# Token tiles of GT in two groups of addresses, with k's results between them

## The chip, the cores and the metric

The kernel runs on one NeuronCore of a Trainium2 chip. TensorE (PE) does the matrix products, VectorE (DVE) and ScalarE (ACT) the element-wise work, GpSimd (POOL) and SyncE (SP) issue transfers between the core's on-chip memory and DRAM, each in the order of its own queue. The metric is the device time of one execution in microseconds, as the median of several runs.

## What is computed

A gated mix of two blocks over 2048 tokens of width 640. The first is a linear attention with 32 heads of 20; the second is a gated linear unit.

```python
x = A_x
g = _sigmoid((x * gate_w).sum(-1, keepdims=True))
a = _A_ref(x, A_wqkv, A_wo)      # linear attention
b = _B_ref(x, B_w_gate, B_w_up, B_w_down)
return g * a + (1 - g) * b

# inside _A_ref
pq, pk = phi(q), phi(k)          # phi(t) = where(t > 0, t + 1, exp(t)) + 1e-6
kv = jnp.einsum("bhsd,bhse->bhde", pk, v)
z = jnp.einsum("bhsd->bhd", pk)
num = jnp.einsum("bhqd,bhde->bhqe", pq, kv)
den = jnp.einsum("bhqd,bhd->bhq", pq, z)[..., None] + 1e-6
o = num / den                    # then o @ wo

# inside _B_ref
h = _sigmoid(x @ w_gate) * (x @ w_up)
return h @ w_down
```

## The kernel before

Every product of two float32 operands is done as three matmuls of a high and a low part (`mm3`, L407 to L409); the parts come from `split`: ACT copies the high part (through `act`, L420) and DVE subtracts it from the source (through `vec2`, L424). All loads and stores go through `Ring.dma_start` (L364), on SP's queue (`sp`) or POOL's (`gp`).

**First stage (pool `p1`).** The keys are made block by block: 8 blocks of two times 128 tokens (`KPlain`, `KBlock`, each with a side 0 and a side 1). ACT and DVE turn a block's product into phi(k) in a tile `kr` or `kb` (`phi_a`, `phi_b`), and POOL adds that tile to `zacc` in memory by an accumulating transfer (`z_add`, L975). `k_split` writes the two parts of phi(k), and `split_xn` the two parts of x, into a *token tile* `tok` of 4 x 640 numbers per partition. Two tiles are used at the start to stage the weights of k (`st`); after them come sixteen token tiles, one for each block and side.

`GTBatch` multiplies x's transpose with phi(k) over a group of token tiles and adds the product to `gt`. The groups are block 0, blocks 1 and 2, blocks 3 and 4, blocks 5 and 6, and, as `glast`, block 7 alone (L1232). The last products of `glast` are the last reads of any token tile; DVE adds them to `gt` (L1245 and L2462).

**Second stage.** `p1` is closed at L1246, and its addresses go to other pools, which are opened with `reuse_waits="tile"`: the first write to a tile waits for the work on those earlier tiles whose bytes it takes, and for no others. On the left, from p1's first byte, comes `mp` (L1545): the operands of M (`wv_sb`, `wo_sb`, `kvt`, `kvh`, `kvl`, `woh`, `wol`). On the right come `pz`, `pw` and `pw2` (L1167, L1248, L1250): the weight tiles of the next products (`ws`, `wu`, `wst`) and their temporaries (`c`, `t`).

SP's queue then issues, in this order: `load_w()` (L1544), which fills a `wst` with the weights ("q", 1, 0); `load_mv(0)`, `load_mv(1)` and `load_mv(2)`, which fill three `wv_sb`; `load_mo(0)`, a `wo_sb`; `load_form(("q", 1, 2), 2)`, a `ws`; `load_mo(1)`, the second `wo_sb`; and `load_form(("q", 1, 2), 1)`, a `wu` (L1640 to L1647). An instruction of SP's queue that waits holds all behind it.

PE goes on with `q_phase(1, ...)` (L2213), which multiplies x with the weights of q in steps. The list `extra` (L2465) hangs other work on these steps: `kv_part(hg)` (L1608) multiplies `wv_sb` with columns of `gt` for a group of heads (L1613, in plain float32), DVE masks the product into `kvt`, `kvh` and `kvl`, and a further `wv_sb` is loaded; `wo_split(hg)` splits a `wo_sb` and loads the one for hg + 2; `m_part(hg)` multiplies both, and the result `ms` is stored to `m_dram` through POOL. `kv_part(0)` and `kv_part(1)` stand right behind the first two steps, whose five products use weights that were loaded earlier. `m_part(4)` takes its result out of PSUM with DVE (`vec_copy`, L860), the others with ACT.

**How the order comes about.** The class `Order` keeps a model of the engines' time while the program is written down, and places the work of ACT and DVE between PE's products. It knows of a tile that its buffer was used before by the tile `bufs` places earlier under the same tag (`place`, L204). It knows nothing of addresses that pools share, except where a line tells it so, such as L1543 and L1641, which set `sp.t`. Each engine then follows its list; semaphores make it wait for what it really needs.

**Where things lie.** The sizes below are bytes per partition and follow from the shapes in the code; the tags of a pool lie in the order in which they first appear. Counted from p1's first byte:

| who | before |
|---|---|
| `ta`, 2 buffers | 0 to 2,624 |
| `kr`, 5 buffers of 2,592 | 2,624 to 15,584 |
| `tok`, 6 buffers of 10,240 | 15,616 to 77,056 |
| `wv_sb` x3, `wo_sb` x2 | 0 to 12,320 |
| `kvt`, `kvh`, `kvl`, `woh`, `wol` | 12,320 to 26,400 |
| `wst`, 2 buffers of 5,120 | 30,976 to 41,216 |
| `ws` of `pw` | 46,336 to 55,552 |
| `wu`, 2 buffers of 3,072 | 55,552 to 61,696 |
| `c`, 5 buffers, and `t`, 4 | 61,696 to 80,128 |

The first three rows are p1's, the others take the same bytes later. At p1's end the six buffers of `tok` hold, in the order of their addresses: block 6 side 0, block 7 side 1, block 7 side 0, block 5 side 1, block 5 side 0, block 6 side 1.

Of the kernel before, what the change touches and what calls it, by code (L numbers as in the profile page):

```python
# [7 lines left out]
F32 = mybir.dt.float32  # L8
F32R = mybir.dt.float32r
# [5 lines left out]
P = 128  # L15
S, D, F = 2048, 640, 1536
# [6 lines left out]
HW = HALF + 2  # L23
# [351 lines left out]
def gated_mix_kernel(ctx: ExitStack, tc: tile.TileContext, xt, xn, wk, wv, wo, wst_q, wst_f, out_t):  # L375
# [111 lines left out]
    p1_cm = tc.tile_pool(name="p1", bufs=1)  # L487
    p1 = p1_cm.__enter__()

    def token_tile(dt=F32R):  # L490
        return p1.tile([P, 4, D], dt, name="tok", tag="tok", bufs=6)

    p1.tile([P, HW], F32, name="first", tag="ta", bufs=2)
    warm = nc.const_aps.tensor(1.0, (P, 512), mybir.dt.bfloat16)
# [179 lines left out]
    chunks = [Chunk(pr, c, xc, 0, xst_v) for pr in range(2) for c in range(TG // CW)]  # L674
    chunks[0].b12 = (b12h, b12l)
    xt_dram = dram.tile([P, 4, 2, 2, CW], F32, name="xt_dram")
    k3h, k3l = (p1.tile([P, 2, HW], F32R, name=n, tag="kr", bufs=5) for n in ("k3h", "k3l"))
    p1.tile([P, 8], F32, name="shift")
    st = [token_tile(F32).rearrange("p a b -> p (a b)") for _ in range(2)]
    wk_st = [st[k // 3][:, k % 3 * 2 * HW:(k % 3 + 1) * 2 * HW] for k in range(KC)]  # L680

    nc.scalar.dma_start(wk_st[0][:, :HW], wk[:P, :HW])
    for k in range(KC):
# [150 lines left out]
    def split_xn(n):  # L834
        i = tok(n // 2, n % 2)
        if i not in TOK:
            TOK[i] = token_tile()
        XN[i] = (TOK[i][:, 0], TOK[i][:, 1])
        split(*XN[i], xn_st.pop(n)[0])
        order.then(lambda: load_xn(n + 3))  # L840
# [118 lines left out]
    def k_split(i, after=""):  # L959
        r = KR.pop(i)  # L960
        if i not in TOK:
            TOK[i] = token_tile()
        PK[i] = (TOK[i][:, 2], TOK[i][:, 3])
        vh, vl = (t.rearrange(view2, j=2) for t in PK[i])
        act(vh, r, AF.Copy, after, bias=EPS)
        at = order.act + A_LAG

        def low():
            order.vec = max(order.vec, at)
            vec3(vl, r, EPS, f32(vh), OP.add, OP.subtract)  # L970
        order.then(low)
# [2071 lines left out]
```

## Time and profile before

| what | value |
|---|---|
| runs shown | 729.92, 731.73 and 733.86 us |
| median of the runs | 731.73 us |
| the profiled execution | 731.62 us |
| its span, first to last instruction | 729.9 us |
| mean granted TensorE clock in it | 0.998 |
| DMA, mean over the span | 263 GB/s, 191.95 MB |

The span is shorter than the profiled execution's time by 1.7 us, which lie around it. Times in the trace count from the span's start. In a timeline a row gives the start, the length, the engine, the line, the operation and its tiles; the bracket at its end is the time that the engine stood idle just before, and what ended that. A line is often that of a helper (L407 to L409, L420, L424, L364), so the tiles tell which work it is. SPq stands for SP's queue, PEld for PE's weight loads.

### The profile page before, as it was taken

The page shows a single profiled execution, that of the slowest core. Times are in us where ns is not written, and L with a number is a line of the kernel's source. Part 1 is how long each engine was busy: PE and PEld are TensorE (multiplying, and loading weights), DVE is VectorE, ACT ScalarE, POOL GpSimd, SP SyncE. Part 2 cuts the span into 40 slices and gives each one's busy share as a digit, 9 for nine tenths or more (in the row PEclk, how much of TensorE's full clock was granted, in tenths as well). Part 3 has the DMA queues.
Part 4 walks back from the last instruction along what each step waited for, and adds up shares of the span by engine and source line. Part 5 has one row for each costly group of instructions (what it writes and reads, how often), then busy time and mean ns, then how long its engine had stood idle before and what let it go on. Part 6 is the DMA issues. An engine that isn't in the chain of part 4 may idle for free.

```text
span 729.9 us, 9895 instructions
## 1 busy us (share of the span) xinstructions
PE 720.1 (99%) x3395; PEld 607.7 (83%) x3395; DVE 587.3 (80%) x1016; ACT 370.6 (51%) x685; POOL 116.9 (16%) x189
## 2 busy tenths in 40 slices
PE   9999999899899999999999999999999999999998
PEld 8999998788688888888888888888888888888886
DVE  6888888975778889898989988347696968799895
ACT  5774749247555763535354855345424241544451
POOL 0211021212310221311111133001010111002300
PEclk9999999999999999999999999999999999999999
DMA  8677679598867866767787979978979895959957
GB/s 253 161 208 202 177 192 287 129 323 284 294 232 269 311 231 241 260 223 263 280 293 287 311 255 336 414 264 268 360 244 293 284 389 180 408 215 336 223 104 237
DMA packets 81961, 191.95 MB, mean 263 GB/s; under 512 B 12234, under 2 KB 40346, under 8 KB 78198
## 3 DMA queue, kind: packets, MB, share of 16 engines
q1 hardware_dynamic: 60726, 117.72, 49.4%
q0 software_dynamic: 20896, 73.36, 30.1%
q8 instruction: 27, 0.44, 0.2%
q10 hardware_dynamic: 288, 0.23, 0.1%
q14 instruction: 24, 0.20, 0.1%
HBM read 113.46 MB, written 75.52 MB: 259 GB/s over the span
## 4 chain that ended last, share of the span: by engine, by line
PE 94%; issue 2%; DMA 1%; DVE 1%; POOL 1%; ACT 1%; SPq 0%; POOLq 0%
PE ch L407 10%; PE ch L409 10%; PE ch L408 10%; PE cc L407 8%; PE cc L409 8%; PE cc L408 8%; PE dd L407 7%; PE dd L408 7%; PE dd L409 7%; PE rot L407 5%; PE rot L409 5%; PE rot L408 5%; DMA wv_sb<-wv 1%; PE dd L2771 1%; PE rot L1613 1%
## 5 line engine op out<-in xcount | busy, mean ns | idle before, releaser
L420 ACT ACTIVATE c<-ch 128x512 f32<-128x512 f32 x54 | 32.2, 596 | 93.9 <-PE ch L409 93.1
L424 DVE TENSOR_TENSOR hf<-c,hf 128x512 fp32r<-128x512 f32 x80 | 54.3, 686 | 19.3 <-ACT hf L420 18.9
L420 ACT ACTIVATE hf<-c 128x512 fp32r<-128x512 f32 x80 | 48.9, 625 | 31.1 <-DVE c L424 31.0
L424 DVE TENSOR_TENSOR c<-cc,c 128x512 f32<-128x512 f32 x42 | 28.9, 687 | 26.7 <-PE cc L409 16.4
L407 PE MATMUL ch<-xth,ws 128*128 128x512 f32 x112 | 43.7, 390 | 0.0
L408 PE MATMUL ch<-xtl,ws 128*128 128x512 f32 x112 | 43.6, 390 | 0.0
L409 PE MATMUL ch<-xth,ws 128*128 128x512 f32 x112 | 43.6, 390 | 0.0
L424 DVE TENSOR_TENSOR c<-c,c 128x512 f32<-128x512 f32 x52 | 35.7, 686 | 3.3 <-ACT c L420 2.7
L424 DVE TENSOR_TENSOR tb<-rot,tb 128x512 f32<-128x512 f32 x56 | 36.0, 680 | 0.3 <-PE rot L409 0.3
L407 PE MATMUL dd<-xrh,wg 128*128 128x512 f32 x90 | 35.4, 393 | 0.0
L408 PE MATMUL dd<-xrl,wg 128*128 128x512 f32 x90 | 35.0, 389 | 0.0
L409 PE MATMUL dd<-xrh,wg 128*128 128x512 f32 x90 | 35.0, 389 | 0.0
L420 ACT ACTIVATE c<-dd 128x512 f32<-128x512 f32 x22 | 13.1, 596 | 41.4 <-PE dd L409 41.4
L407 PE MATMUL cc<-xbh,ws 128*128 128x512 f32 x84 | 32.9, 392 | 0.5 <-DVE c L424 0.5
L408 PE MATMUL cc<-xbl,ws 128*128 128x512 f32 x84 | 32.7, 389 | 0.0
L409 PE MATMUL cc<-xbh,ws 128*128 128x512 f32 x84 | 32.7, 389 | 0.0
L424 DVE TENSOR_TENSOR tb<-dd,tb 128x512 f32<-128x512 f32 x36 | 24.7, 685 | 9.3 <-PE dd L409 9.3
L420 ACT ACTIVATE dd<-ch 128x512 f32<-128x512 f32 x22 | 12.8, 582 | 35.9 <-PE ch L409 35.9
L424 DVE TENSOR_TENSOR tb<-cc,tb 128x512 f32<-128x512 f32 x36 | 24.4, 682 | 1.9 <-PE cc L409 1.9
L424 DVE TENSOR_TENSOR wst<-wst 128x256 f32<-128x256 f32 (+1 forms) x65 | 24.6, 395 | 1.4
L409 PEld LDWEIGHTS ch<-xth,ws 128*128 128x128 f32 x112 | 21.0, 188 | 4.7 <-DVE ws L424 0.3
L408 PEld LDWEIGHTS ch<-xtl,ws 128*128 128x128 f32 x112 | 21.0, 188 | 4.3
(690 smaller groups left out, 2333.2 us busy)
## 6 DMA issues: line engine op xcount, KB each, us to landing
wf<-ws POOLq DMA_DIRECT2D x12, 1152.0 KB, 7.5
ws<-wf SPq DMA_DIRECT2D x11, 1152.0 KB, 8.6
wst<-wst_f SPq DMA_DIRECT2D x12, 640.0 KB, 4.9
wf<-wg POOLq DMA_DIRECT2D x12, 640.0 KB, 6.8
wd<-wd POOLq DMA_DIRECT2D x12, 640.0 KB, 7.8
wg<-wf SPq DMA_DIRECT2D x12, 640.0 KB, 6.8
wf<-wd SPq DMA_DIRECT2D x10, 640.0 KB, 10.9
xnst<-xn SPq DMA_DIRECT2D x16, 320.0 KB, 5.1
```

The source lines that it names most:

```text
L407: nc.tensor.matmul(out, l_hi, r_hi, start=first, stop=False, skip_group_check=True)
L408: nc.tensor.matmul(out, l_hi, r_lo, start=False, stop=False, skip_group_check=True)
L409: nc.tensor.matmul(out, l_lo, r_hi, start=False, stop=last, skip_group_check=True)
L420: nc.scalar.activation(out, src, fn, **kw)
L424: nc.vector.tensor_tensor(out, a, b, op=op)
L1613: nc.tensor.matmul(ps[:w, :w], v[:, m, :w], gt[:, m, c0:c0 + w], start=(m == 0), stop=(m == KC - 1))
L2771: nc.tensor.matmul(ps, l, r, start=new, stop=j == 1 and k == ks[-1], skip_group_check=True)
```

## The change

The token tiles get two tags instead of one. Of six in turn, the first four take the tag `toka` with four buffers, the other two the tag `tokb` with two buffers. In the order of the tiles the last six are blocks 5, 6 and 7 with two sides each; blocks 5 and 6 fall to `toka`, block 7 to `tokb`. Two tiles that only take up room change: `shift` grows from 32 to 192 bytes and is placed ahead of `toka`, and `space` of 1,888 bytes stands behind `kr`.

```diff
+    tok_n = []
+
     def token_tile(dt=F32R):
-        return p1.tile([P, 4, D], dt, name="tok", tag="tok", bufs=6)
+
+        early = len(tok_n) % 6 < 4
+        tok_n.append(0)
+        return p1.tile([P, 4, D], dt, name="tok", tag="toka" if early else "tokb", bufs=4 if early else 2)
...
-    k3h, k3l = (p1.tile([P, 2, HW], F32R, name=n, tag="kr", bufs=5) for n in ("k3h", "k3l"))
-    p1.tile([P, 8], F32, name="shift")
+    p1.tile([P, 48], F32, name="shift")
     st = [token_tile(F32).rearrange("p a b -> p (a b)") for _ in range(2)]
     wk_st = [st[k // 3][:, k % 3 * 2 * HW:(k % 3 + 1) * 2 * HW] for k in range(KC)]
+    k3h, k3l = (p1.tile([P, 2, HW], F32R, name=n, tag="kr", bufs=5) for n in ("k3h", "k3l"))
+    p1.tile([P, 472], F32, name="space")
```

Counted again from p1's first byte, its tiles then lie as follows; those of the later pools stay where they are.

| who | after |
|---|---|
| `ta` | 0 to 2,624 |
| `toka`, 4 buffers of 10,240 | 2,816 to 43,776 |
| `kr`, 5 buffers of 2,592 | 43,776 to 56,736 |
| `space` | 56,736 to 58,624 |
| `tokb`, 2 buffers of 10,240 | 58,624 to 79,104 |

`p1` ends 2,048 bytes higher, and with it the pool `qs` that stands on it.

## The prediction

> **What bounds the kernel now.** The page comes first, for the share of each engine and for the chain that ended last:
>
> ```profile
> span 729.9 us, 9895 instructions
> PE 720.1 (99%) x3395; PEld 607.7 (83%) x3395; DVE 587.3 (80%) x1016; ACT 370.6 (51%) x685; POOL 116.9 (16%) x189
> PE 94%; issue 2%; DMA 1%; DVE 1%; POOL 1%; ACT 1%; SPq 0%; POOLq 0%
> ```
>
> TensorE is busy 99% of the span and is 94% of the chain, so the change can win only what PE waits. The view of waits for PE alone, over the whole span, is short (engine, line, what it waited for: us in total, times, longest):
>
> ```profile
> PE dd L407 <- DVE ms L860: 2.4, 1, 2.4
> PE rot L1613 <- DMA wv_sb<-wv: 2.3, 1, 2.3
> PE rot L497 <- PEq L3034: 0.8, 1, 0.8
> PE cc L407 <- DVE c L424: 0.5, 1, 0.5
> PE dd L407 <- DVE c L424: 0.4, 1, 0.4
> ```
>
> One of the two large waits is for a load, `wv_sb`, the first operand of M. The chain in order of time shows what released it (start, length, what), and the timelines of PE and of SP's queue show the same stretch:
>
> ```profile
> 140.18 0.33 SPq L364
> 140.56 5.22 DMA wv_sb<-wv
> 145.82 3.88 PE rot L1613 x20
> ```
> ```profile
> 131.28 0.28 PE L409 MATMUL rot<-tok 128*128 128x256 f32 x1
> ...
> 139.76 0.39 PE L409 MATMUL cc<-tok 128*128 128x512 f32 x1
> ...
> 145.82 3.88 PE L1613 MATMUL rot<-gt,wv_sb 128*120 128x120 f32 x20 [2.28 <-DMA wv_sb<-wv]
> ```
> ```profile
> 120.60 0.34 SPq L364 DMA_DIRECT2D w<-wst_q  x1
> 140.18 0.33 SPq L364 DMA_DIRECT2D wst<-wst_q  x1
> 140.56 1.91 SPq L364 DMA_DIRECT2D wv_sb<-wv  x3
> 142.56 1.92 SPq L364 DMA_DIRECT2D wo_sb<-wo  x1
> 144.53 0.50 SPq L364 DMA_DIRECT2D ws<-wq  x1
> 145.12 0.41 SPq L364 DMA_DIRECT2D wo_sb<-wo  x1
> 145.59 0.41 SPq L364 DMA_DIRECT2D wu<-wq  x1
> ```
>
> SP issues nothing from 120.94 to 140.18. It then issues `wst` 0.03 us after PE's last matmul on a token tile ends (139.76 + 0.39 = 140.15). That tile is the last group's (block 7, the two tiles of `glast`). `wst`'s bytes lie inside one of them, and the six loads behind it stand in the same in-order queue. `wv_sb` lands at 145.78; PE had come to it at 145.82 - 2.28 = 143.54.
>
> The wait has a second price, in the granted clock of these stretches (length, busy time and count of PE, PEld, DVE, ACT, POOL, then PEclk, DMA share, GB/s):
>
> ```profile
> 130.00:140.00 10.00, 10.00 (x56) 8.80 (x55) 9.86 (x17) 0.00 (x0) 3.00 (x3) 1.00 0.42 66
> 146.00:148.00 2.00, 2.00 (x13) 2.00 (x13) 0.62 (x2) 0.08 (x1) 0.00 (x0) 0.59 1.22 243
> 148.00:150.00 2.00, 2.00 (x11) 1.96 (x11) 1.58 (x5) 0.00 (x0) 0.32 (x1) 0.55 1.14 214
> 180.00:190.00 10.00, 7.08 (x34) 5.45 (x33) 8.45 (x19) 5.55 (x11) 3.83 (x7) 1.00 0.68 228
> ```
>
> Right behind the wait PE ran at 0.59 and 0.55 of its clock for 2 us each: (1 - 0.59) x 2 + (1 - 0.55) x 2 = **1.72 us** lost. Loads and clock together cost PE 2.28 + 1.72 = 4.00 us here.
>
> **The change part by part.** No instruction is added or removed, and the planner sees the same ring (with groups of four and two, tile i still follows tile i - 6). So every engine's order stays; what changes is which old tile a load waits for.
>
> *The three loads of M, `wst` and the first `wo_sb`.* By the sizes in the code, `wst`'s first buffer takes bytes 30,976 to 36,096 behind p1's start, and M's operands the bytes below 26,400. After the change these are toka's (2,816 to 43,776): blocks 5 and 6, which PE last reads in the group before `glast`, ending at 131.28 + 0.28 = 131.56. Block 7 is in tokb, from 58,624 on. So `wst` can go at about 131.6, 8.6 us earlier, and the first `wv_sb` 0.38 us behind it as now: 132.0, and with the 5.22 us of its row it lands at 137.2, or 6.3 us before PE comes. Bounds of that landing: 5.22 us was measured with the DMA engines full, and they are at 0.42 in 130:140; even at 11.5 us PE would not wait. What is late next is `gt`, written by DVE:
>
> ```profile
> 141.35 1.27 DVE L424 TENSOR_TENSOR gt<-cc,gt 128x512 f32<-128x512 f32 x2
> ...
> 147.80 0.28 DVE L424 TENSOR_TENSOR kvt<-rot,bd 120x120 f32<-120x120 f32 x1 [1.38 <-issue]
> ...
> 149.74 0.28 DVE L424 TENSOR_TENSOR kvt<-rot,bd 120x120 f32<-120x120 f32 x1 [0.35 <-PE rot L1613]
> ...
> 152.35 0.83 DVE L424 TENSOR_TENSOR wol<-wo_sb,woh 120x640 fp32r<-120x640 f32 x1 [1.16 <-ACT woh L420]
> ...
> 157.78 0.69 DVE L428 SCALAR_TENSOR_TENSOR qe<-qe,qr 128x512 f32<-128x512 f32 x1 [0.19 <-ACT qr L420]
> ...
> 161.07 0.68 DVE L424 TENSOR_TENSOR xtl<-xz,xth 128x512 fp32r<-128x512 f32 x1
> ```
>
> `gt` is complete at 142.62, 0.92 us before PE needs it at 143.54. The 2.28 us go.
>
> *The clock.* A halved stretch (1.72 us lost at half rate are 3.4 us) began behind this wait, so I take it to go with the wait: 1.72 us, bounds 0 and 1.72.
>
> [...] The trace doesn't settle it: a longer wait inside 180:190 left the clock at 1.00.
>
> *What DVE lets PE keep.* PE's next wait is already there, 0.39 us for DVE; the second row is the 2.4 us one:
>
> ```profile
> 164.04 0.41 PE L407 MATMUL dd<-woh,kvh 120*120 120x320 f32 x1 [0.39 <-DVE c L424]
> ...
> 185.05 0.39 PE L407 MATMUL dd<-woh,kvh 100*100 100x320 f32 x1 [2.45 <-DVE ms L860]
> ```
>
> DVE's idle between `gt` and that instruction's chain (through `xtl` at 161.07) is 1.38 + 0.35 + 1.16 + 0.19 = **3.08 us**, and the timeline shows no other of weight. If all its inputs come 4 us earlier, DVE moves up by 3.08 and no more. So PE comes 4.00 earlier, waits 0.39 + 0.92 instead of 0.39, and keeps 3.08. The inputs do come: the 1.16 is ACT's wait for the first `wo_sb`, issued at 142.56 now and near 134.0 then.
>
> ```profile
> 151.59 0.74 ACT L420 ACTIVATE woh<-wo_sb 120x640 fp32r<-120x640 f32 x1 [5.51 <-DMA wo_sb<-wo]
> ...
> 175.79 0.74 ACT L420 ACTIVATE woh<-wo_sb 100x640 fp32r<-100x640 f32 x1 [2.54 <-DMA wo_sb<-wo]
> ```
>
> *The wait that is added.* k's results (kr) now lie at bytes 43,776 to 56,736, under `ws` (46,336 to 55,552) and the first `wu`. So `ws` must wait for POOL's last accumulates that read kr, and the second `wo_sb` and `wu` are queued behind it:
>
> ```profile
> 130.04 1.21 POOL L364 DMA_DIRECT2D zacc<-kr  x1 [7.99 <-DVE xbl L424]
> 134.70 1.19 POOL L364 DMA_DIRECT2D zacc<-kb  x1 [3.45 <-DVE gt L424]
> ```
>
> and the view of the tile `zacc` between 125 and 145 us gives for both
>
> ```profile
> DMA to landing us min/median/max: 4.1/4.1/4.1
> ```
>
> The last one lands at 134.70 + 4.1 = 138.8. `ws` then goes at 138.8 rather than 144.53, still 5.7 us earlier, and all behind it too. The queue behind is free again before anybody wants it: cost nothing, covered by that 5.7 us.
>
> *The second wait (2.45 us at 185.05).* It goes back to DVE, and behind DVE to ACT's 2.54 us for the fifth `wo_sb`:
>
> ```profile
> 167.53 1.75 SPq L364 DMA_DIRECT2D wo_sb<-wo  x2
> ```
>
> From issue to ACT's use are 175.79 - 167.53 = 8.26 us. All of that chain moves up with DVE (3.08), so at the same crowding the wait stays 2.45. With some 2 MB of loads moved into 131 to 140, the engines have less waiting when it is issued. Bounds: 0 and 2.45 less. I take **1.0**, nearer to none, since the stores issued just before it move along with it.
>
> **Sum.** 3.08 + 1.0 = 4.1 us. The profiled run took 731.62 (span 729.9 and 1.7 around it): 731.62 - 4.1 = **727.5 us**. The median shown is 731.73, from 729.92 to 733.86, so the profiled run is a middle one; half-clock stretches that come or stay away (1.72 each) would explain that spread, though no row shows it. Behind 190 us PE waits for nothing, and the engines that feed it wait for PE, so I let the gain reach the end.
>
> **The rivals.**
>
> *The halved clock moves to the second wait.* That wait remains at 1.4 to 2.5 us, and a wait of 2.28 was followed by a halved stretch while one of 2.45 wasn't, so chance has a part in it. Price 1.72: 729.3.
>
> *The second wait closes too.* If the fifth `wo_sb` comes 2.45 earlier: 731.62 - 3.08 - 2.45 = 726.1. For it: ACT's 2.54 there is all DMA. Against: the share in 180:190 is only 0.68, so crowding isn't all of it.
>
> *The halved clock was no child of the wait.* Then PE gains 2.28 only, less than DVE's 3.08, and with the 1.0 it is 728.3. Against: the rest of this span ran at 1.00 in every stretch quoted.
>
> *Given back.* The loads of M wait less, but later loads (1.22 and 1.14 of the DMA engines are taken in 146 to 150) hold DVE back by the whole gain before 185: 731.6. The same time comes out if the load still shares bytes with a block 7 tile, which the sizes exclude unless the buffers are handed out otherwise.
>
> *Slower: the new wait for the accumulates.* Between 100 and 200 us the landings of `zacc` spread:
>
> ```profile
> DMA to landing us min/median/max: 4.1/5.9/8.5
> ```
>
> Each waits for the one before. With the early loads beside them at 8.5 us each, they land at 138.5 and 147.0; `ws` goes 2.5 us later than now, and the second `wo_sb` and `wu` with it. It decides from a landing past 144.5. ACT's second `woh` and all behind it slip by up to 2.5, PE with them: 734.1, and 735.8 with one more halved stretch. Against: 4.1 is what both took here, and the DMA share there is 0.42.
>
> **How the numbers follow.** Chances: forecast 0.42 (its own range 726.3 to 728.6); clock at the second wait 0.22; second wait closed 0.13; clock unrelated 0.08; given back 0.11; slower 0.04. Range **725.4 to 730.8**: forecast and first three rivals, which hold 0.85, with some 1 us at each end for the spread between runs, which can also throw a run out. A measurement can tell about 0.5% (3.7 us) from no change, so faster means below 728.1: most of the forecast and the closed case, **0.49**; slower means above 735.4: **0.03**; between: **0.48**.
>
> **What would show each step.** SP's `wst` near 131.6 and `wv_sb` behind it; no PE wait before L1613, whose twenty matmuls then take some 2 us; PEclk 1.00 in the 4 us behind; `ws` near 139, released by a `zacc` landing; the wait for DVE c grown to about 1.3; the one for DVE ms between 0 and 2.5. The prediction is wrong if `wst` still goes at PE's last token matmul, if `gt` or ACT holds L1613 instead, or if the wait at ms grows by what was won.

## The result, and the profile after

| | before | after |
|---|---|---|
| first comparison, median (range), 6 runs each | 732.28 us (729.92 to 733.86) | 726.51 us (725.35 to 729.87) |
| ratio after/before, 95% interval | | 0.993 (0.9902 to 0.9957) |
| repeated, median (range) | 731.64 us (730.30 to 732.69), 17 runs | 726.48 us (726.21 to 726.93), 5 runs |
| ratio, 95% interval | | 0.993 (0.9917 to 0.9943) |

The change makes the kernel about 0.7% faster: 5.2 us in the larger comparison. The forecast was 727.5 us.

The page of the first profiled run after (729.87 us, the slowest of its six), with the chain's shares last:

```profile
span 728.0 us, 9897 instructions
PE 719.7 (99%) x3395; PEld 607.4 (83%) x3395; DVE 587.0 (81%) x1016; ACT 370.5 (51%) x685; POOL 116.4 (16%) x189
PE 90%; DVE 4%; issue 2%; DMA 2%; POOL 1%; ACT 0%; SPq 0%; DVEq 0%; POOLq 0%; ACTq 0%
```

The same engines do the same work, but DVE's share of the chain rose from 1% to 4%: between 130 and 150 us the chain now runs over DVE. SP's queue in that run:

```profile
132.77 0.33 SPq L364 DMA_DIRECT2D wst<-wst_q  x1
133.15 1.56 SPq L364 DMA_DIRECT2D wv_sb<-wv  x3
134.76 1.99 SPq L364 DMA_DIRECT2D wo_sb<-wo  x1
142.22 0.37 SPq L364 DMA_DIRECT2D ws<-wq  x1
142.64 0.43 SPq L364 DMA_DIRECT2D wo_sb<-wo  x1
```

`wst` no longer waits for block 7: it goes 7.4 us earlier than before, and with it the three `wv_sb` and the first `wo_sb`. `ws`, the first load over k's results, and the two loads behind it go 2.3 to 2.5 us earlier. (Behind `wst` stand seven loads, and not six as the prediction has it.) From the view of PE's waits the one new row of weight, and PE's timeline:

```profile
PE ch L407 <- ACT kb L420: 0.9, 1, 0.9
```
```profile
144.56 2.26 PE L1619 MATMUL rot<-gt,wv_sb 128*120 128x120 f32 x20
...
161.54 0.41 PE L407 MATMUL dd<-woh,kvh 120*120 120x320 f32 x1 [0.87 <-DVE c L424]
...
182.33 0.39 PE L407 MATMUL dd<-woh,kvh 100*100 100x320 f32 x1 [2.25 <-DVE ms L866]
```

The wait for `wv_sb` is gone, and the twenty matmuls of L1619 (L1613 before) take 2.26 us instead of 3.88. The wait for DVE's tile `c` grew from 0.39 to 0.87; the wait for its tile `ms`, called the second wait here, is nearly what it was. The clock is the column before the last two:

```profile
130.00:140.00 10.00, 10.00 (x57) 9.03 (x56) 9.86 (x17) 0.00 (x0) 1.96 (x2) 1.00 0.86 191
146.00:148.00 2.00, 2.00 (x14) 1.79 (x14) 1.97 (x5) 2.00 (x5) 0.83 (x2) 1.00 1.02 350
148.00:150.00 2.00, 2.00 (x10) 1.65 (x10) 1.90 (x7) 0.82 (x2) 0.56 (x1) 1.00 1.04 258
180.00:190.00 10.00, 7.75 (x30) 6.34 (x30) 8.05 (x16) 4.77 (x10) 3.84 (x7) 0.83 0.71 234
```

It is whole at 146 to 150, and 0.83 in 180:190: in this run (1 - 0.83) x 10 = 1.7 us were lost behind the second wait. The new wait for `kb`, far ahead of the change's place (at 109.96), delays everything behind it; the chain leads from it back to a load of `qraw` that took 5.80 us. Without the two, 729.87 - 0.9 - 1.7 = 727.3, among the other five runs, which all had a clock of 1.000.

### The profile page after: what moved, and what is told of

Same layout as the page of the kernel before. It is cut to its first block, busy times and chain, and to the rows that moved or that the text cites. A ratio compares the mean times of both kernels' runs of the same rounds, so it can differ in the third digit from the quotient of the medians.

```text
span 728.0 us, 9897 instructions
## 1 busy us (share of the span) xinstructions
PE 719.7 (99%) x3395; PEld 607.4 (83%) x3395; DVE 587.0 (81%) x1016; ACT 370.5 (51%) x685; POOL 116.4 (16%) x189
## 4 chain that ended last, share of the span: by engine, by line
PE 90%; DVE 4%; issue 2%; DMA 2%; POOL 1%; ACT 0%; SPq 0%; DVEq 0%; POOLq 0%; ACTq 0%
PE ch L407 10%; PE ch L409 10%; PE ch L408 10%; PE cc L407 8%; PE cc L408 8%; PE cc L409 8%; PE dd L407 6%; PE dd L408 6%; PE dd L409 6%; PE rot L407 5%; PE rot L409 5%; PE rot L408 5%; DMA qraw<-wst_f 1%; DVE xtl L424 1%; DVE gt L424 1%
```

## The experiments

Four questions are put: whether the gain is the earlier start of SP's queue; whether DVE sets how much of it PE keeps; what the second wait hangs on; and what the clock costs.

**The kernel after once more,** to see what in its first profile was chance.

> The kernel after, unchanged. The profiled run of after had a transfer early in it (the second qraw, issued at 101.51) that took 5.80 us where before it took 3.78, a new wait of PE of 0.9 us for kb, and a half-clock stretch behind the wait for ms (183.8 to 187.2). If both are chance: time 726 to 727.5, the wait for kb mostly gone in a new profile, and the clock at 1.00 behind the second wait in some executions and 0.5 in others. If the layout causes the wait for kb, it shows again with 0.9 us.

726.48 us; the clock is 1.000 in all five runs, and no wait for `kb` shows. Two kernels below do show one: the first try at undoing the early start (1.0 us, new addresses) and the kernel before with three buffers (1.3 us, old addresses). So the new addresses don't cause it; it comes and goes by chance. PE in the new profile, a run of 726.93 us:

```profile
143.25 2.26 PE L1619 MATMUL rot<-gt,wv_sb 128*120 128x120 f32 x20
...
160.24 0.41 PE L407 MATMUL dd<-woh,kvh 120*120 120x320 f32 x1 [0.87 <-DVE c L424]
...
180.37 0.39 PE L407 MATMUL dd<-woh,kvh 100*100 100x320 f32 x1 [1.61 <-DVE ms L866]
```

Set against the rows of before, this splits the whole difference of the two profiled runs, 731.62 - 726.93 = 4.69 us. PE is ready for L1619 at 143.25 instead of 143.54 (0.29, ahead of the change's place, and so no part of its effect); the product at `c` starts 3.80 earlier, so 3.51 come between the two; the product at `ms` starts 4.68 earlier, so 0.88 more come there, nearly all from the shorter wait (2.45 - 1.61 = 0.84). Behind it nothing changes.

**Old addresses, `wst` issued behind the three `wv_sb`.** The queue's head is taken away without moving a tile.

```diff
+    eng, late = sp.engine, []
+    sp.engine = type("Late", (), {"dma_start": lambda self, o, s: late.append((o, s))})()
     load_w()
+    sp.engine = eng
...
     load_mv(2)
+    for o, s in late:
+        eng.dma_start(o, s)
     load_mo(0)
```

> The kernel before with its old addresses; only the transfer of wst is issued behind the three loads of wv_sb instead of ahead of them. Theory (the whole loss comes from wst standing at the head of SP's in-order queue, whatever the addresses): the first wv_sb goes before 135 us and lands before 143, the wait for wv_sb and the half clock behind it go; the other two wv_sb wait for the last accumulates of k (near 139), wst goes near 140.2 and wo_sb right behind it, so ACT's first woh still waits some us and DVE keeps more of its idle: 728.5 to 730.5, a ratio of 0.995 to 0.998. Rival (the new addresses are needed for any gain): as before, 1.000, with a wait of 2 us or more for wv_sb.

728.41 us (727.30 to 729.84, 6 runs), just below the expected range, and a ratio of 0.9957 (0.9945 to 0.9970): 3.2 of the 5.2 us, with not one address changed, and a clock of at least 0.999 in all six runs. SP's queue, and PE's waits:

```profile
120.98 19.47 SPq L364 DMA_DIRECT2D wv_sb<-wv  x3
140.56 0.63 SPq L1648 DMA_DIRECT2D wst<-wst_q  x1
```
```profile
PE dd L407 <- DVE c L424: 1.5, 1, 1.5
PE dd L407 <- DVE ms L860: 1.1, 1, 1.1
PE cc L407 <- DVE kvt L424: 0.9, 1, 0.9
```

The first `wv_sb` went at once, the other two waited until some 139.5 for the accumulates that read k's results (the last was issued at 135.3 and took 4.1 us to land). PE waits for no load, but for DVE: 0.9 at `kvt` and 1.5 at `c`, where the repeated after has 0.87 at `c` and none at `kvt`. The expectation had put the remaining loss on ACT's `woh`; the timelines of ACT and DVE show another tile, `wst`, which now comes late itself:

```profile
147.86 0.74 ACT L420 ACTIVATE wg<-wst 128x640 fp32r<-128x640 f32 x1 [2.95 <-DMA wst<-wst_q]
```
```profile
148.63 0.83 DVE L424 TENSOR_TENSOR wg<-wst,wg 128x640 fp32r<-128x640 f32 x1 [1.47 <-ACT wg L420]
```

The queue's order was the cause of the wait; what the addresses add is that all the loads come early.

**New addresses, the first `wo_sb` late:** issued behind `ws`.

```diff
+    eng, late = sp.engine, []
+    sp.engine = type("Late", (), {"dma_start": lambda self, o, s: late.append((o, s))})()
     load_mo(0)
+    sp.engine = eng
     load_form(("q", 1, 2), 2)
+    for o, s in late:
+        eng.dma_start(o, s)
```

> The kernel after; only the first wo_sb is issued behind ws instead of ahead of it, near 142.6 as it was before the change. Theory (what PE keeps is set by DVE, and DVE by ACT's woh, which waits for the first wo_sb): no wait for wv_sb, clock 1.00 in 140 to 150, but ACT waits some 4 to 5 us for wo_sb, DVE gets an idle of about 1 us behind it and PE's wait for c grows by about that: 0.8 to 1.3 us slower than after, some 727.5 to 728. Rival (PE's own wait and the clock behind it are the whole price, the first wo_sb has room): as after within 0.3 us.

728.93 us (726.81 to 732.35, 12 runs), a ratio of 0.9968 (0.9954 to 0.9982). The theory had the direction, but missed the size (727.5 to 728 was expected) and the way. The wait for `c` is 0.9 as in after: `wo_sb` went at 140.38 and ACT began with it at 146.59, 6.2 us later (9.0 before, when everything came at once), and that was soon enough. What grew is the other wait, and half a clock behind it:

```profile
PE dd L407 <- DVE ms L866: 2.7, 1, 2.7
PE dd L407 <- DVE c L424: 0.9, 1, 0.9
```
```profile
183.00:184.00 1.00, 1.00 (x4) 0.71 (x4) 1.00 (x3) 0.00 (x0) 0.18 (x1) 0.50 0.59 216
```

Seven of the twelve runs have a mean clock below 0.999. Why the later wait grew with the first `wo_sb` late isn't shown.

**New groups, but k's results at the lowest addresses,** with the low group above them.

```diff
+    k3h, k3l = (p1.tile([P, 2, HW], F32R, name=n, tag="kr", bufs=5) for n in ("k3h", "k3l"))
     p1.tile([P, 48], F32, name="shift")
...
-    k3h, k3l = (p1.tile([P, 2, HW], F32R, name=n, tag="kr", bufs=5) for n in ("k3h", "k3l"))
     p1.tile([P, 472], F32, name="space")
```

> The kernel after with the token tiles in the two groups, but k's results lie at the lowest addresses as before, with the low group above them and the free bytes behind it. Theory (the split of the token tiles frees wst, but M's operands now lie over k's results, so the second and third wv_sb and the first wo_sb wait for the last accumulates of k, landing at 139 to 142): the first wv_sb is early, PE waits 0 to 2.5 us for the second or third or ACT for wo_sb: 0.3 to 2 us slower than after, 726.8 to 728.5. Rival (the place of k's results does not matter, only the split): as after within 0.3 us.

728.01 us (727.13 to 729.33, 6 runs), a ratio of 0.9955 (0.9943 to 0.9968). The number is the theory's; the profile shows only half of its way:

```profile
130.83 7.97 SPq L364 DMA_DIRECT2D wv_sb<-wv  x3
```

The second and third `wv_sb` do wait for the accumulates, until some 138 by an estimate from the row's end at 138.80, but PE waits for neither, and its wait for `c` is 0.9 as in after. The wait at `ms` is 2.2, 0.6 more than in the repeated after; two of six runs had a clock of 0.998. The two profiled runs, 727.90 and 726.93 us, differ by only 0.3 in their spans (725.5 and 725.2); the other 0.7 lies outside the span. So most of the 1.5 us between the medians stays unexplained.

**Undoing the early start, first try:** one small transfer at the head of the queue, into a buffer that should lie over block 7.

```diff
+    nc.sync.dma_start(tt("hold")[:1, :8], xn[:1, :8])
     load_w()
```

> The kernel after with one small transfer (8 numbers) put ahead of wst in SP's queue, into a t buffer whose bytes lie over a token tile of block 7: the queue's head again waits for the last products of glast, with the new addresses otherwise kept. Theory (the early start of the queue is the whole gain): wst near 140.5, PE waits 2 us or more for wv_sb, a half-clock stretch behind it in most executions, 730.5 to 732.5 us, a ratio of 0.998 to 1.002. Rival (the new addresses bring something of their own, for instance the loads behind ws): 726.5 to 729.

728.01 us (726.34 to 731.71, 12 runs), a ratio of 0.9957 (0.9940 to 0.9974). It wasn't the undo that was meant: as the first tile of its pool the buffer took the place of `ws`, over k's results, and moved the other tiles of that pool. SP's queue shows it:

```profile
137.53 0.30 SPq L1550 DMA_DIRECT2D hold<-xn  x1
137.94 0.36 SPq L364 DMA_DIRECT2D wst<-wst_q  x1
```

It is let go at 137.53 and not at 140. In the profiled run (727.55 us) PE still doesn't wait for `wv_sb`; but the median is 1.5 us above the repeated after, five of twelve runs show a clock of 0.998, and three take over 730.8 us. An estimate: with the 5.22 us that the first `wv_sb` of before took from issue to landing, the first one of this run, issued at 138.35, lands near 143.6; PE came to it at 143.93 here and at 143.25 in the repeated after. So a start at 138 leaves hardly any room, and other runs may wait; no profile here shows one that does.

**Three buffers of `wo_sb` in the kernel after.** The second wait follows one transfer. For the fifth `wo_sb`, from SP's and ACT's timelines and PE's waits:

| kernel | issued | ACT begins | issue to use | PE's wait at `ms` | difference |
|---|---|---|---|---|---|
| before | 167.53 | 175.79 | 8.26 | 2.45 | 5.81 |
| after | 165.02 | 173.06 | 8.04 | 2.25 | 5.79 |
| after, repeated | 163.73 | 171.11 | 7.38 | 1.61 | 5.77 |
| old addresses, `wst` late | 165.62 | 172.47 | 6.85 | 1.09 | 5.76 |
| first `wo_sb` late | 162.92 | 171.40 | 8.48 | 2.70 | 5.78 |
| k low | 163.43 | 171.39 | 7.96 | 2.19 | 5.77 |

In these six profiles every microsecond that this transfer takes beyond 5.8 is a microsecond of PE.

```diff
-            o = mp.tile([bdn, D], F32, name="wo_sb", tag="wo_sb", bufs=2)
+            o = mp.tile([bdn, D], F32, name="wo_sb", tag="wo_sb", bufs=3)
...
-        order.then(lambda: load_mo(hg + 2))
+        order.then(lambda: load_mo(hg + 3))
...
+    load_mo(2)
```

> The kernel after with three wo_sb buffers instead of two, so that the fifth wo_sb is loaded one wo_split earlier. In six profiles the wait for ms was the fifth wo_sb's time from issue to landing minus 5.75 us (8.23 and 2.45, 7.36 and 1.61, 6.83 and 1.09, 8.45 and 2.70). Theory (that landing is the whole second wait): the wait for ms falls below 0.5 us, no half clock in any run, 724.3 to 725.3. Rival (DVE's own backlog ends the wait too, or the earlier load holds up ws and the second wo_sb): the wait stays above 1 us, or the wait for c grows by it; 726 to 727.

725.33 us (725.06 to 725.42, 6 runs), a ratio of 0.9905 (0.9887 to 0.9923), the upper edge of what was expected. It has the lowest median here, 1.15 us below the repeated after; each against the runs of before beside it, 6.1 us are won instead of 5.2. Its waits:

```profile
PE dd L407 <- DVE c L424: 0.9, 1, 0.9
PE rot L502 <- PEq L3041: 0.8, 1, 0.8
PE cc L407 <- DVE c L424: 0.5, 1, 0.5
PE dd L407 <- DVE ms L866: 0.4, 1, 0.4
```

The landing was the second wait: 1.6 went to 0.4. The runs lie within 0.4 us of each other, and none has a clock below 0.999.

**Three buffers of `wo_sb` in the kernel before.** The same edit on the old addresses.

> The kernel before with three wo_sb buffers. Theory (the two waits are independent, and the half clock of every run of before hangs on the first): the wait for wv_sb of 2 to 2.5 us and a clock of 0.997 to 0.998 stay, the wait for ms goes: 728.8 to 730, a ratio of 0.996 to 0.998. Rival (the second wait is where the clock is lost in many runs): the clock rises to 0.999 or 1.0 and the time falls to 727.5 to 728.5. Third (DVE is late from the first wait on, so a new wait takes the place): 731 to 732.

729.56 us (728.46 to 730.53, 10 runs), a ratio of 0.9964 (0.9952 to 0.9977): 1.9 us less, so the second wait is a saving of its own, as the first theory says. Its word on the clock held in half of the runs only: five are at 1.000, with a median of 729.53, and five at 0.997 to 0.998, with 729.62. Of the 56 runs of before beside the experiments 49 lie below 0.999, so some of their half clocks may have come behind the second wait; the mean of a run doesn't tell the place. The profiled run, at 1.000, is the slowest of the ten and has the wait for `kb`, so the two medians don't give the price of a stretch either. PE in the profiled run, and its clock:

```profile
147.39 2.44 PE L1613 MATMUL rot<-gt,wv_sb 128*120 128x120 f32 x20 [2.51 <-DMA wv_sb<-wv]
...
164.77 0.41 PE L407 MATMUL dd<-woh,kvh 120*120 120x320 f32 x1 [1.06 <-DVE c L424]
```
```profile
148.00:150.00 2.00, 2.00 (x19) 1.96 (x18) 1.14 (x4) 0.00 (x0) 0.00 (x0) 1.00 1.12 228
```

The wait of 2.51 us was followed by no half clock this time. From the start of L1613 until PE was ready for the product at `c` it took 16.32 us, where before took 17.83: with the clock whole, 1.51 less. PE then waited 1.06 for `c` instead of 0.39, so DVE took 0.67 of that, and 0.84 was kept.

**Undoing the early start, second try:** the buffer for the small transfer is taken where no later tile moves to another place.

```diff
+    pw.tile([P, 2, 9 * P], F32R, name="ws", tag="ws"), wu_tile(), wu_tile(), [ct("c") for _ in range(5)]
+    nc.sync.dma_start([tt("hold") for _ in range(4)][0][:1, :8], xn[:1, :8])
     load_w()
```

> The kernel after with one small transfer (8 numbers) ahead of wst in SP's queue, into a t buffer over a token tile of block 7, with all later tiles at their addresses of after (in the earlier try the later tiles had moved, and the transfer lay over k's results, so the queue was let go at 137.5, when the last accumulate had landed). Theory: wst near 140.4, the first wv_sb lands near 145.8, PE waits about 2.3 us for it, the clock is below 1.0 in most executions, and the wait for c falls back to 0.4 to 1.1: 730.5 to 732, the time of before. Rival (part of the gain comes from the addresses and not from the earlier issue): below 729.5.

730.61 us (728.36 to 732.99, 12 runs) against 731.86 of before beside it (730.11 to 735.66, 18 runs), a ratio of 0.9979 (0.9963 to 0.9996). SP's queue, and PE's waits:

```profile
139.71 0.30 SPq L1551 DMA_DIRECT2D hold<-xn  x1
140.07 0.36 SPq L364 DMA_DIRECT2D wst<-wst_q  x1
```
```profile
PE rot L1621 <- DMA wv_sb<-wv: 2.5, 1, 2.5
PE dd L407 <- DVE ms L866: 2.3, 1, 2.3
...
PE dd L407 <- DVE c L424: 0.4, 1, 0.4
```
```profile
146.00:148.00 2.00, 2.00 (x12) 2.00 (x12) 0.00 (x0) 0.00 (x0) 0.00 (x0) 0.50 1.18 220
```

The picture of before is back: the wait of 2.5, half a clock behind it (in ten of twelve runs the mean clock is 0.997 or 0.998), and 0.4 at `c`. Some 4 of the 5.2 us go with the early start. About 1.3 us stay (the interval gives 0.3 to 2.7), with the addresses or with a queue that starts 0.1 us sooner; the runs don't tell which.

**Old addresses, `wst` late, three buffers.**

> The kernel before with its old addresses, wst behind the three wv_sb, and three wo_sb buffers. Theory (the loads ahead of 140 us are what the new addresses bring beyond the queue's order: with the old ones the first wo_sb lands near 148.6 and DVE passes that on to PE as waits for kvt and c of 2.4 us together, which stay): the wait for ms falls to 0.4, 727 to 728. Rival (those waits give way too, and the addresses bring nothing beyond the queue's order): 725 to 726, as the kernel after with three buffers.

727.02 us, a ratio of 0.9942 (0.9922 to 0.9962), but from 725.37 to 730.69 in seven runs. The median is the theory's number; the profiled run (725.97 us) shows what the rival said, with no wait for `kvt` and 0.9 for `c`. It stays unclear. What can be said is that the order of the queue with a third buffer gets near the best time in some runs, while the new addresses with three buffers get there in all six.

## Why the prediction was nearly right

**The queue.** Right. `wst` was forecast at 131.6 and went at 131.46 in the repeated profile (132.77 in the first). The load is ahead of PE, and the 2.28 us went. The second undo shows that most of the gain lies here.

**The clock.** It went with the wait in most runs: after has a mean clock of 0.999 or more in 10 of 11 runs, before in 7 of 56, and the second undo, which brings the wait back, in 2 of 12. So the rival "no child of the wait" falls. But the wait alone doesn't decide it, as the kernel before with three buffers shows (5 of 10). In the profiles here a half clock (0.50 at its lowest) came behind waits of 2.28, 2.55, 2.25 and 2.70 us; waits of 2.45, 2.51, 2.19 and 2.3 us were followed by none (a clock of 1.00), nor, between 130 and 200 us, was any of 1.61 or less.

What picks among waits of like length, no run shows.

What one lost stretch costs depends on what comes behind it. Of the 56 runs of before beside the experiments, the medians by mean clock are:

| mean clock | runs | median |
|---|---|---|
| 0.999 or more | 7 | 730.79 |
| 0.997 to 0.998 | 39 | 731.59 |
| 0.991 to 0.995 | 10 | 732.87 |

The step from the first row to the second, about one stretch of 1.7 us in the clock, costs 0.8 there, and not 1.72, as the prediction had it for the spread between runs: without it PE would have waited longer for DVE at `c`, as the profile with three buffers shows (0.84 kept of 1.51). Behind the second wait less seems to hide it: with the first `wo_sb` late, where PE waits for no load, the runs at 0.997 to 0.998 have a median of 729.34 and those above of 727.78, 1.6 more. These are five runs each, and their ranges overlap.

**What DVE lets PE keep.** Right in kind: PE came to `c` 4.0 us earlier (143.54 to 163.65 before, 143.25 to 159.37 after; 20.11 and 16.12), waited for DVE there, and kept what DVE had made up. The size was off: 3.08 was forecast, 3.51 came, and so the wait for `c` grew to 0.87 and not to the 1.3 of the forecast. The sum of DVE's idle as the brackets give it was too small. DVE's chain from `gt` to the last `xtl` in the repeated after:

```profile
141.21 1.28 DVE L424 TENSOR_TENSOR gt<-cc,gt 128x512 f32<-128x512 f32 x2
...
150.41 0.55 DVE L424 TENSOR_TENSOR wu<-wst,wu 128x384 fp32r<-128x384 f32 x1
150.88 0.68 DVE L428 SCALAR_TENSOR_TENSOR qe<-qe,qr 128x512 f32<-128x512 f32 x1
...
157.27 0.68 DVE L424 TENSOR_TENSOR xtl<-xz,xth 128x512 fp32r<-128x512 f32 x1
```

and the same two instructions of before:

```profile
153.70 0.55 DVE L424 TENSOR_TENSOR wu<-wst,wu 128x384 fp32r<-128x384 f32 x1
154.38 0.69 DVE L428 SCALAR_TENSOR_TENSOR qe<-qe,qr 128x512 f32<-128x512 f32 x1
```

From `gt` to `xtl` are 16.06 us now and were 161.07 - 141.35 = 19.72: 3.66 less. In the rows of after, instructions that don't wait overlap: `qe` starts 0.47 behind `wu`, which takes 0.55. Before it started 0.68 behind it; that is 0.21 lost with no bracket. Each of the four brackets leaves an overlap of some 0.08 out as well. With these, 3.08 becomes 3.6.

**The wait that is added.** It costs PE nothing, as forecast, but the landing was mis-sized: 4.1 us was forecast for the last accumulate, as in before. Both accumulates of `zacc` in the first profile after:

```profile
DMA to landing us min/median/max: 4.1/6.0/7.9
```

The second shared the engines with the early loads (0.86 busy in 130:140 instead of 0.42), so `ws` went at 142.22 and not at 138.8; in the repeated profile it went at 141.11. It was half-way to the rival that ends slower: of the cover of 5.7 us, 2.3 and 3.4 were left.

**The second wait.** This step failed in part. The forecast was a wait shorter by 1.0, from more room for the fifth `wo_sb`. The repeated after has 0.84 less, the first 0.20 less: the transfer took 7.4 and 8.0 us from issue to use, not 7.3. The cause was read rightly; that this transfer alone sets the wait, and that its length varies from run to run, only the later profiles show.

**The sum.** 4.1 was forecast for the profiled run; 4.69 came, as 0.29 + 3.51 + 0.88. DVE's term was 0.43 too small and that of the second wait 0.12 too large, and the 0.29 from ahead of the change is luck. The median of 726.48 is 0.45 below that profiled run, the slowest of its five. So the measured 726.5 lies nearer to the rival "second wait closes" (726.1), but not by its way, since that wait stays at 1.6 to 2.25. The rival of the half clock at the second wait happened in the first profiled run; the other ten of the eleven have a clock of 1.000. Nothing was given back later.

## What to carry to other kernels

Look at what stands at the head of an in-order queue, and which old bytes its destination takes: with the tiles moved, the head and four of the seven loads behind it went 7 us or more earlier here, and moving the one transfer alone let the load that PE waited for go at once (at 120.98 and not at 140.56). What the removed wait was worth was set by the next engine in line (PE came to `c` 4.0 us earlier and kept 3.5, what DVE had made up), so follow its chain from start to start of its instructions, not by adding up its marked idle. A wait that is a transfer's duration less a constant in every profile (5.8 us in six here) is that transfer's; an earlier issue, with one more buffer, took it from 1.6 to 0.4 us, and on the new addresses the runs then lay within 0.4 us.

## What was not expected of the hardware

A wait of TensorE of 2.19 to 2.70 us was followed by a stretch at half clock (0.50 at its lowest) in four of eight profiled cases, and its length doesn't tell in which: at the same instruction a wait of 2.28 was, and one of 2.51 wasn't. The accumulating transfer took 4.1 us from issue to landing where the DMA engines were 0.42 busy, and 7.9 and 7.6 us beside the early loads (0.86 and 1.02 busy).
